# Block products for the second of eight batches, with the weights kept in DRAM one batch earlier, in an attention and gated feed-forward kernel

## The chip, the cores and the metric

The kernel runs on one core of a Trainium2 chip. The metric is device time in microseconds: the median of repeated executions of the whole program. TensorE (PE in the profile) does matrix products; VectorE (DVE), ScalarE (ACT) and GpSimd (POOL) work elementwise; SyncE (SP) issues the transfers. SBUF is the on-chip memory, PSUM holds TensorE's results in eight banks.

## What is computed

```
def sm_attn(qq, kk, vv):
    s = scale * np.matmul(qq, kk.transpose(0, 1, 3, 2))
    s = s - np.max(s, axis=-1, keepdims=True)
    a = np.exp(s)
    a = a / (np.sum(a, axis=-1, keepdims=True) + 1e-09)
    return np.matmul(a, vv)
p_packed = sm_attn(p, k, v)
attn_out = sm_attn(q, p_packed, p_packed)
x = attn_out.transpose(0, 2, 1, 3).reshape(B * S, H * D)
a = x @ w_a
b = x @ w_b
out = a * b @ w_out
```

There are 8 batches with 8 heads, 576 positions of 64 features each, 32 packed queries per head, and 512 x 1536, 512 x 1536 and 1536 x 512 weights. All data are float32.

## The kernel before

**The algebra.** The second attention's output is a2 (softmax weights, 256 rows per batch: 8 heads x 32 packed positions) times the packed values. So x @ w_a is a2 times G, where G is the packed values times w_a, and likewise for w_b. The kernel makes G (`g_tiles` or `make_g`), multiplies it with a2 (the first product, giving a and b), multiplies a by b to h, and multiplies h with w_out (the second product).

**Words.** Each float32 operand is split into a high part of type fp32r and a low part (`lo_part`, line 93: value minus high part). A product takes three passes: high x high, high x low, low x high. So for G, for a2, for h and for w_out there are tiles named `_hi`, written by ScalarE, and `_lo`, written by VectorE or GpSimd.

**Feature tiles.** The 1536 features are 12 tiles (`NFT`) of 128. For one tile and one batch the *plain* first product (`mm1`, `mm1_half`, line 406) is 24 matmuls of 288 columns. The *block* first product (`product`, line 790, and `period`, line 844) gets the same a and b from seven products of half size, three passes each: 21 matmuls of 288 columns. It needs sums and differences of the blocks of G (`make_g`, line 801; `split_g`, line 829) and of a2 (`half_sum`, line 631, steps t0 to t3 on GpSimd; `half_parts`, line 638, steps u0 to u3 on ScalarE and VectorE). The low words of the sums of a2 are `tx_lo`.

**Stages.** Batches 0 and 1 (`NB = 2`, line 56) use the plain first product, batches 2 to 7 the block one. While batch b's first product runs, the attention of batch b + 1 runs in between: `stage1` (steps S, r) and `stage2` (steps s), in an order written out by hand in strings. `START` orders the steps ahead of batch 0's first product, `PLAN_0` those beside batch 0, `PLAN` those beside batch 1, `STEPS` those beside later batches, one entry per place in a period.

**Weights.** w_a, w_b and w_out arrive as raw 64-bit pairs of words in batch 0 and are put together in three steps: A (`high_word`, ScalarE), B (`low_word`, on the engine that `WAYS` names), C (`both_words`, line 212, VectorE, the join). Step D splits a piece of w_out into its two parts. w_a and w_b stand together in the tile `w_ab` in SBUF, 6 chunks of 1 MB, while batches 0 and 1 use them. `keep_weights` (line 624) writes the chunks to DRAM (`w_kept`), three near the end of batch 0 and three in batch 1. From batch 2 on `load_kept` (line 730) reads one chunk for two feature tiles into `wr`.

**A block period.** Period n ends tile n and begins tile n + 1 in two pairs of PSUM banks, X and V:

```
product(n, 5, X), product(n + 1, 1, X), product(n + 1, 2, V)
ScalarE copies X to d; fillers; VectorE adds V to d
product(n, 3, X), product(n + 1, 6, X)
ScalarE copies X to c2; VectorE multiplies X by d: half of h; fillers
product(n, 4, V), product(n + 1, 7, V)
VectorE adds c2 to V, multiplies by d: the other half of h; fillers
```

The fillers are matmuls of a second product (`mm2_steps`, line 749), taken from a list in the numbers that `FILLS` gives (three numbers per period). They stand where the next product waits for the copy or the sum.

**Second products before.** Batch 0's second product (4 output tiles x 12 feature tiles x 3 passes = 144 matmuls, `mm2_part`) follows its first product as a block, lines 691 to 711: nine feature tiles first, the last three behind. Batch 1's (180 matmuls, 5 output tiles) begins with a block of 96 right behind its plain first product and is otherwise filler in batch 2's periods. The memory of `w_ab` and of the plain G (pool `plain`) is released at line 712, and the tiles of the block periods (pool `late`) take its place.

**The start.** `wake` (lines 588 to 592) runs matmuls of zeros in between, so that TensorE has work while the first weights arrive.

## Time and profile before

| What | Value |
|---|---|
| Median of 3 runs | 708.7 us (707.92 to 709.09) |
| Profiled execution, first to last instruction | 705.6 us |
| TensorE busy | 699.4 us, 99% |
| VectorE busy | 455.9 us, 65% |
| GpSimd busy | 417.1 us, 59% |
| ScalarE busy | 356.9 us, 51% |
| DMA moved | 102.65 MB, mean 145 GB/s |
| Chain that ended last | 91% TensorE, 4% VectorE |

The profiled execution is one run of the program; its own time in the profile is the span. Busy time is the union of an engine's instructions. Matmuls overlap (one begins before the one ahead has ended), so their durations add up to more than the time they take; the chain of waits gives groups of them with the time that the group advances. The named idle time of an engine is what it waited just before an instruction, and for whom.

### The profile page before, as it was taken

How to read it: one execution, taken by the hardware profiler on the slowest of the kernel's cores; microseconds unless marked ns; L12 is line 12 of the kernel's file. 1: busy time of each engine (PE TensorE's matmuls, PEld its weight loads, DVE VectorE, ACT ScalarE, POOL GpSimd, SP SyncE). 2: the span in 40 equal slices, each digit the busy share in tenths (PEclk: the TensorE clock that was granted, in tenths of full speed). 3: DMA queues.
4: the chain of work that ended last, by engine and by line, in shares of the span. 5: the costliest groups of instructions: out<-in, count | busy, mean ns of one | idle time of the engine just before them, and what ended most of it. 6: DMA issues, size and time to landing. Idle time of an engine off the chain costs nothing.

```text
span 705.6 us, 14386 instructions
## 1 busy us (share of the span) xinstructions
PE 699.4 (99%) x5654; PEld 582.8 (83%) x5654; DVE 455.9 (65%) x833; ACT 356.9 (51%) x719; POOL 417.1 (59%) x321
## 2 busy tenths in 40 slices
PE   9999999999999999999999999999999999999998
PEld 7888878898788888878888788888888878888886
DVE  4997765467365679566775678765785667754332
ACT  3778724554244555535554455554545446544520
POOL 1596741337254777646863589566775578856520
PEclk9999999999999999999999999999999999999999
DMA  9999986753254736356434664556145323133002
GB/s 316 380 229 297 282 233 136 252 106 93 69 141 161 170 89 172 115 139 168 119 95 124 173 161 95 131 165 173 63 123 154 106 91 119 60 124 117 1 1 75
DMA packets 179460, 102.65 MB, mean 145 GB/s; under 512 B 145728, under 2 KB 161344, under 8 KB 174016
## 3 DMA queue, kind: packets, MB, share of 16 engines
q1 hardware_dynamic: 179392, 101.73, 50.7%
q8 instruction: 44, 0.72, 0.4%
q14 instruction: 24, 0.20, 0.1%
HBM read 85.98 MB, written 15.73 MB: 144 GB/s over the span
## 4 chain that ended last, share of the span: by engine, by line
PE 91%; DVE 4%; issue 1%; DMA 1%; ACT 1%; SPq 1%; DVEq 0%
PE x L754 36%; PE m L796 28%; PE m L414 11%; PE m L440 5%; PE x L810 4%; PE s L326 2%; PE s L341 1%; PE x L396 1%; PE s L280 1%; DMA qn<-in_q_dram 1%; PE s L316 1%; DVE a_lo L93 1%; DVE part L764 0%; DVE d L878 0%; DVE w_ab L212 0%
## 5 line engine op out<-in xcount | busy, mean ns | idle before, releaser
L754 PE MATMUL x<-wo,h_hi 128*128 128x512 f32 (+1 forms) x776 | 249.4, 391 | 0.0
L93 POOL TENSOR_TENSOR h_lo<-asb,h_hi 128x576 fp32r<-128x576 f32 x95 | 139.0, 1465 | 76.0 <-ACT h_hi L841 42.8
L754 PEld LDWEIGHTS x<-wo,h_hi 128*128 128x128 f32 x776 | 140.8, 188 | 22.1 <-ACT part L762 0.8
L754 PE MATMUL x<-wo,h_lo 128*128 128x512 f32 (+1 forms) x388 | 152.2, 392 | 0.0
L93 POOL TENSOR_TENSOR G_lo<-gs,G_hi 128x640 fp32r<-128x640 f32 x72 | 113.1, 1577 | 29.6 <-ACT G_hi L831 29.4
L754 PEld LDWEIGHTS x<-wo,h_lo 128*128 128x128 f32 x388 | 72.9, 188 | 11.7
L93 POOL TENSOR_TENSOR A_lo<-gs,A_hi 128x256 fp32r<-128x256 f32 x36 | 27.2, 755 | 89.3 <-ACT A_hi L819 89.3
L878 DVE TENSOR_TENSOR d<-m,d 128x576 f32<-128x576 f32 (+1 forms) x73 | 54.1, 741 | 34.7 <-ACT d L874 33.9
L891 DVE TENSOR_TENSOR asb<-m,d 128x288 f32<-128x288 f32 x72 | 32.5, 451 | 63.2 <-ACT c L887 59.9
L887 ACT COPY c<-m 128x288 f32<-128x288 f32 x72 | 28.8, 400 | 82.5 <-PE m L796 82.5
L764 DVE TENSOR_TENSOR part<-x,part 128x512 f32<-128x512 f32 (+1 forms) x65 | 44.1, 678 | 38.8 <-PE x L754 38.8
L796 PE MATMUL m<-tx_hi,G_hi 128*128 128x288 f32 x216 | 63.8, 296 | 0.0
L796 PE MATMUL m<-tx_hi,G_lo 128*128 128x288 f32 x216 | 63.6, 295 | 0.0
L796 PE MATMUL m<-tx_lo,G_hi 128*128 128x288 f32 x216 | 63.2, 293 | 0.0
L816 ACT COPY gs<-x 128x512 f32<-128x512 f32 x35 | 20.6, 588 | 82.2 <-PE x L810 80.6
L831 ACT CAST G_hi<-gs 128x640 fp32r<-128x640 f32 x72 | 52.2, 729 | 15.7 <-POOL gs L825 15.1
L874 ACT COPY d<-m 128x576 f32<-128x576 f32 (+1 forms) x73 | 46.7, 640 | 19.2 <-PE m L796 18.8
L841 ACT CAST h_hi<-asb 128x576 fp32r<-128x576 f32 x72 | 49.0, 680 | 11.5 <-DVE asb L905 11.5
L796 PEld LDWEIGHTS m<-a_hi,G_hi 128*128 128x128 f32 x144 | 27.0, 187 | 31.9 <-issue 17.4
L825 POOL TENSOR_TENSOR gs<-gs 128x512 f32<-128x512 f32 x36 | 46.7, 1297 | 3.2 <-DVE gs L822 2.9
L796 PE MATMUL m<-a_hi,G_hi 128*128 128x288 f32 x144 | 46.6, 324 | 0.0
L904 DVE TENSOR_TENSOR m<-m,c 128x288 f32<-128x288 f32 x72 | 33.3, 463 | 17.0 <-PE m L796 15.3
(189 smaller groups left out, 1568.9 us busy)
## 6 DMA issues: line engine op xcount, KB each, us to landing
wr<-w_kept SPq DMA_DIRECT2D x36, 1024.0 KB, 5.1
nat<-in_k_dram SPq DMA_DIRECT2D x56, 144.0 KB, 4.7
nat<-in_q_dram SPq DMA_DIRECT2D x56, 144.0 KB, 5.3
vt<-in_v_dram SPq DMA_DIRECT2D x28, 256.0 KB, 3.9
out_dram<-part SPq DMA_DIRECT2D x27, 256.0 KB, 2.1
raw<-in_moe_w_a_dram SPq DMA_DIRECT2D x12, 512.0 KB, 8.7
raw<-in_moe_w_b_dram SPq DMA_DIRECT2D x12, 512.0 KB, 8.7
raw<-in_moe_w_out_dram SPq DMA_DIRECT2D x12, 512.0 KB, 6.9
```

Source lines behind the costliest of these rows:

```text
L93: return eng.tensor_tensor(out=dst, in0=src, in1=hi.bitcast(F32), op=ALU.subtract)
L414: nc.tensor.matmul(out=ps[:, half, 0:HS], lhsT=gt[:, kt, ft % 4, cols], rhs=at[:, kt, HS * half:HS * half + HS], start=(n == 0 and kt == 0 ...
L440: nc.tensor.matmul(out=o[:, cols], lhsT=ht[:, c0:c0 + P], rhs=wt[:, cols], start=(ft == 0 and n == 0), stop=(ft == NFT - 1 and n == 2))
L754: nc.tensor.matmul(out=o[:, cols], lhsT=ht[:, c0:c0 + P], rhs=wt[:, cols], start=(ft == fts[0] and n == 0), stop=end)
L764: nc.vector.tensor_tensor(out=parts[i][:, cols], in0=o[:, cols], in1=parts[i][:, cols], op=ALU.add)
L796: nc.tensor.matmul(out=bank[:, n % 2, 0:HS], lhsT=g, rhs=t, start=(first and i == 0), stop=(i == 2), skip_group_check=True)
L825: nc.gpsimd.tensor_tensor(out=gs[:, 2:4].rearrange("p a u f -> p a (u f)"), in0=gs[:, 0:2].rearrange("p a u f -> p a (u f)"), in1=s2.unsqu ...
L831: nc.scalar.copy(out=G_hi[:, n % 3], in_=gs[:, 1:6, n % 2])
L841: nc.scalar.copy(out=view(h_hi[ft]), in_=src)
L874: nc.scalar.copy(out=d[:, both], in_=X[:, both, 0:HS])
L878: nc.vector.tensor_tensor(out=d[:, both], in0=V[:, both, 0:HS], in1=d[:, both], op=ALU.add)
L904: nc.vector.tensor_tensor(out=v, in0=v, in1=c2, op=ALU.add)
```

## The change

`NB` becomes 1: batch 1 too goes through block periods, so there are seven batches of 12 block tiles. The rest follows from that:

- `w_ab` becomes six tiles. Chunks 0 and 1 lie in a pool of their own (`kp`); block periods of batch 1 use them in place (tags A and wr) and later put the parts of G's blocks (`A`) and the loaded chunks (`wr`) in their memory. Chunks 2 to 5 lie in the pool `plain`, whose memory the late tiles take.
- All six chunks are written to DRAM in batch 0, by steps K0 to K5 of `PLAN_0`.
- Batch 0's second product is nine feature tiles as a block, whose sums ScalarE copies out (`put_part`); its last three feature tiles (36 matmuls) become the first fillers.
- Batch 1's block periods get tables of their own: `STEPS_1`, and `FIRST_FILLS` for periods -2 to 11. Periods -2 and -1 begin the first tile.
- In batch 1, `GLO` and `HLO_1` put 6 of the 12 low parts of G and 5 of those of h on VectorE; the others stay on GpSimd.
- `START`, `WAYS`, `SUBS`, `MULS`, `WLO` and `PLAN_0` get other contents; the order of the first loads changes (a first weight load ahead of q's second part and of v).

```
-    NB = 2
+    NB = 1
+    kp = ep(tc.tile_pool(name="kp", bufs=1, side="right"))
...
-    w_ab = plain_p.tile([P, NC, R, 4 * P], F32, name="w_ab")
+    w_ab = [kp.tile([P, R, 4 * P], F32, name=f"w_ab{c}", tag=("A", "wr")[c]) for c in range(2)]
+    w_ab += [plain_p.tile([P, R, 4 * P], F32, name=f"w_ab{c}") for c in range(2, NC)]
...
-    SUBS, MULS, LOWS = "0101", "0100", "01"
-    HLO, WLO = "000000001000", "000011000011"
+    SUBS, MULS, LOWS = "0110", "1010", "01"
+    HLO, WLO = "000000001000", "010010000101"
...
+            elif name[0] == "K":
+                keep_weights(int(name[1]))
...
-        if n < LAST:
-            t = lp.tile([P, R, 4 * P], F32, name="wr")
+        if n < 4:
+            wr_of[n] = w_ab[n // 2]
+        elif n < LAST:
+            t = kp.tile([P, R, 4 * P], F32, name="wr", tag="wr")
...
-        lo_part(G_lo[:, n % 3], gs[:, 1:6, n % 2], G_hi[:, n % 3], nc.gpsimd)
+        lo_part(G_lo[:, n % 3], gs[:, 1:6, n % 2], G_hi[:, n % 3], nc.vector if GLO[n:n + 1] == "1" else nc.gpsimd)
...
-            lo_part(view(h_lo[ft]), src, view(h_hi[ft]), nc.gpsimd)
+            lo_part(view(h_lo[ft]), src, view(h_hi[ft]), nc.vector if HLO_1[n:n + 1] == "1" else nc.gpsimd)
...
+    F0 = 9
+    tiles = list(enumerate(tiles_of(0)))
+    pairs = [bank_pair() for _ in range(2)]
+    banks = [pairs[i % 2][:, i // 2, :] for i in range(4)]
+    for f in range(F0):
+        for i in (1, 3, 0, 2):
+            drain(mm2_steps(banks[i], tiles[i][1], [f], None, first=f == 0, last=f == F0 - 1))
+            if i in (3, 2):
+                between()
+    for i in (1, 3, 0, 2):
+        put_part(0, 0, banks[i], i, 0)
...
+    def rest_of_first():
+        for i, c0 in tiles:
+            o = bank()
+            yield from mm2_steps(o, c0, range(F0, NFT), lambda o=o, i=i, c0=c0: put_part(0, 2, o, i, c0))
+    filler[0] = rest_of_first()
...
+    GLO, HLO_1 = "101100001110", "000011010101"
+    FIRST_FILLS = ((0, 8, 6), (0, 4, 0), (4, 1, 2), (2, 0, 0), (2, 0, 2), (2, 1, 0), (0, 0, 0), (2, 0, 0), (11, 3, 8), (9, 5, 0), (6, 1, 7), (5, 5, 0), (6, 0, 14), (14, 2, 0))
...
     for n in (-2, -1):
-        period(n, (12, 12, 12), STEPS[n])
+        period(n, FIRST_FILLS[n + 2], STEPS[n])
```

**What moves, at three places.** The rows are instructions in the order in which an engine takes them; L and a number is the line in the kernel at hand, and the names left of the arrow are written, those right of it read.

The first place is TensorE at the changeover to block products, period -1: products 1 and 2 of the first tile, then what comes ahead of product 6 (`tx_hi`). Before (first tile of batch 2, two rows of the block ahead of it):

```order
L754 MATMUL x<-wo,h_hi_518 128x512 x2
L754 MATMUL x<-wo,h_lo_519 128x512
L796 MATMUL m<-a_hi,A_hi 128x288
L796 MATMUL m<-a_hi,A_lo 128x288
L796 MATMUL m<-a_lo,A_hi 128x288
L796 MATMUL m<-a_hi,A_hi 128x288
L796 MATMUL m<-a_hi,A_lo 128x288
L796 MATMUL m<-a_lo,A_hi 128x288
L754 MATMUL x<-wo,h_hi_520 128x512 x2
L754 MATMUL x<-wo,h_lo_521 128x512
L754 MATMUL x<-wo,h_hi_522 128x512 x2
L754 MATMUL x<-wo,h_lo_523 128x512
```

And now (first tile of batch 1):

```order
L686 MATMUL x<-wo,h_hi_540 128x512 x2
L729 MATMUL m<-a_hi,A 128x288 x2
L729 MATMUL m<-a_lo,A 128x288
L729 MATMUL m<-a_hi,A 128x288 x2
L729 MATMUL m<-a_lo,A 128x288
L729 MATMUL m<-tx_hi,G_hi 128x288
L729 MATMUL m<-tx_hi,G_lo 128x288
L729 MATMUL m<-tx_lo,G_hi 128x288
L686 MATMUL x<-wo,h_lo_541 128x512
```

Before, 12 fillers stood between products 2 and 6; now product 6 follows directly, and the fillers ahead of product 1 are 14 of batch 0's 36.

The second place is TensorE in period 2 of the first block batch, from the fillers behind product 2 to those at its end: products 3 (`a_hi`), 6 (`tx_hi`), 4 (`tx_hi`) and 7. Before:

```order
L754 MATMUL x<-wo,h_hi_520 128x512 x2
L754 MATMUL x<-wo,h_lo_521 128x512
L754 MATMUL x<-wo,h_hi_522 128x512 x2
L796 MATMUL m<-a_hi,G_hi 128x288
L796 MATMUL m<-a_lo,G_hi 128x288
L796 MATMUL m<-a_hi,G_lo 128x288
L796 MATMUL m<-tx_hi,G_hi 128x288
L796 MATMUL m<-tx_lo,G_hi 128x288
L796 MATMUL m<-tx_hi,G_lo 128x288
L316 MATMUL s<-ident,t_2495 128x128 x4
L317 MATMUL s<-ident,t_2495 64x128
L754 MATMUL x<-wo,h_lo_523 128x512
```

And now:

```order
L686 MATMUL x<-wo,h_hi_538 128x512 x2
L729 MATMUL m<-a_hi,G_hi 128x288
L729 MATMUL m<-a_lo,G_hi 128x288
L729 MATMUL m<-a_hi,G_lo 128x288
L729 MATMUL m<-tx_hi,G_hi 128x288
L729 MATMUL m<-tx_lo,G_hi 128x288
L729 MATMUL m<-tx_hi,G_lo 128x288
L729 MATMUL m<-tx_hi,G_hi 128x288
L729 MATMUL m<-tx_lo,G_hi 128x288
L729 MATMUL m<-tx_hi,G_lo 128x288
```

Two fillers are left behind product 2, and none stands between product 6 and product 4.

The third place is VectorE in period 0 of the first block batch, from one add of d to the next. Before:

```order
L878 TENSOR_TENSOR d<-m,d 128x576
L286 TENSOR_REDUCE nmx<-s 128x1
L287 TENSOR_SCALAR nmx<-nmx 128x1
L891 TENSOR_TENSOR asb<-m,d 128x288
L904 TENSOR_TENSOR m<-m,c_2372 128x288
L905 TENSOR_TENSOR asb<-m,d 128x288
L764 TENSOR_TENSOR part_2225<-x,part_2225 128x512
L878 TENSOR_TENSOR d<-m,d 128x576
```

And now:

```order
L813 TENSOR_TENSOR d<-m,d 128x576
L826 TENSOR_TENSOR asb<-m,d 128x288
L839 TENSOR_TENSOR m<-m,c_1589 128x288
L840 TENSOR_TENSOR asb<-m,d 128x288
L95 TENSOR_TENSOR G_lo<-gs,G_hi 128x640
L306 TENSOR_SCALAR rs<-rs,rs_1682 128x1
L307 RECIPROCAL rs<-rs 128x1
L813 TENSOR_TENSOR d<-m,d 128x576
```

The low part of G, which GpSimd made before, stands in VectorE's queue ahead of the next add of d.

## Rows read from the trace of the kernel before

**Rows 1.** The page, part 1: busy time, share of the span and instructions.
```profile
PE 699.4 (99%) x5654; PEld 582.8 (83%) x5654; DVE 455.9 (65%) x833; ACT 356.9 (51%) x719; POOL 417.1 (59%) x321
```

**Rows 2.** By stage: length; busy PE, PEld, DVE, ACT, POOL; clock; DMA share, GB/s.
```profile
28.20:80.60 52.40, 51.38 (x493) 43.61 (x492) 44.48 (x71) 40.64 (x74) 41.80 (x25) 1.00 0.97 297
80.60:118.30 37.70, 37.70 (x255) 28.60 (x253) 26.35 (x41) 16.02 (x28) 16.02 (x11) 1.00 0.76 190
118.30:167.10 48.80, 48.80 (x542) 43.69 (x541) 26.21 (x45) 24.46 (x47) 19.25 (x14) 1.00 0.60 148
...
275.00:358.00 83.00, 82.94 (x647) 69.26 (x640) 57.16 (x109) 43.71 (x91) 55.93 (x45) 1.00 0.50 134
```

**Rows 3.** Chain of waits in order of time: start us, us, what.
```profile
149.75 1.60 PE m L414 x12
...
185.99 2.78 PE x L754 x12
...
192.53 1.20 PE x L810 x16
...
215.44 1.20 PE m L796 x9
```

**Rows 4.** Groups by line, VectorE from 80.6 to 118.3: busy us, mean ns, idle before.
```profile
L212 DVE SCALAR_TENSOR_TENSOR wo_f<-raw 128x512 uint32<-128x512 uint32 x8 | 5.4, 681 | 3.2 <-POOL wo L93 2.9 <-POOL raw L206 0.2
L126 DVE STREAM_TRANSPOSE xT<-nat 128x1152 f32<-128x1152 f32 x3 | 4.0, 1348 | 0.0
L206 DVE TENSOR_SCALAR raw<-raw 128x512 uint32<-128x512 uint32 x5 | 3.2, 663 | 0.0
L93 DVE TENSOR_TENSOR wo<-wo_f,wo 128x512 fp32r<-128x512 f32 x4 | 2.9, 734 | 2.1 <-ACT wo L237 2.1
...
L366 DVE STREAM_TRANSPOSE t<-t 128x576 f32<-128x576 f32 x2 | 1.5, 774 | 1.4 <-POOL t L362 1.4
```

**Rows 5.** Groups by line over the whole span, same columns.
```profile
L93 POOL TENSOR_TENSOR h_lo<-asb,h_hi 128x576 fp32r<-128x576 f32 x95 | 139.0, 1465 | 76.0 <-ACT h_hi L841 42.8 <-ACT h_hi L433 32.3
L93 POOL TENSOR_TENSOR G_lo<-gs,G_hi 128x640 fp32r<-128x640 f32 x72 | 113.1, 1577 | 29.6 <-ACT G_hi L831 29.4
...
L878 DVE TENSOR_TENSOR d<-m,d 128x576 f32<-128x576 f32 x71 | 53.2, 749 | 30.3 <-ACT d L874 29.5
...
L874 ACT COPY d<-m 128x576 f32<-128x576 f32 x71 | 45.9, 646 | 15.9 <-PE m L796 15.5
...
L891 DVE TENSOR_TENSOR asb<-m,d 128x288 f32<-128x288 f32 x72 | 32.5, 451 | 63.2 <-ACT c L887 59.9 <-POOL G_lo L93 1.4 <-POOL h_lo L93 0.7
...
L822 DVE TENSOR_TENSOR gs<-gs,x 128x256 f32<-128x256 f32 x35 | 14.7, 421 | 1.2
```

**Rows 6.** Instructions on tiles a_lo and h_lo: duration ns min/median/max, first and last start.
```profile
L93 DVE TENSOR_TENSOR a_lo<-t,a_hi x25: 444/1036/1726, 110.1 to 607.0; 128x288 fp32r<-128x288 f32 x24, 128x576 fp32r<-128x576 f32 x1
...
L93 DVE TENSOR_TENSOR h_lo<-asb,h_hi x1: 759/759/759, 69.0 to 69.0; 128x576 fp32r<-128x576 f32 x1
```

**Rows 7.** Timeline of VectorE from 262 us: start us, us, instruction.
```profile
268.89 1.94 DVE L93 TENSOR_TENSOR tx_lo<-tf,tx_hi 128x576 fp32r<-128x576 f32 x1
...
273.65 1.73 DVE L93 TENSOR_TENSOR a_lo<-t,a_hi 128x288 fp32r<-128x288 f32 x1
...
276.16 0.45 DVE L93 TENSOR_TENSOR a_lo<-t,a_hi 128x288 fp32r<-128x288 f32 x1
```

**Rows 8.** Timeline of GpSimd in the same stretch.
```profile
273.51 1.55 POOL L93 TENSOR_TENSOR G_lo<-gs,G_hi 128x640 fp32r<-128x640 f32 x1
```

**Rows 9.** Chain of waits from 0 to 36 us.
```profile
22.24 2.49 DVE w_ab L212 x4
...
30.62 0.49 ACT ghi L402
...
31.16 3.72 PE m L414 x24
```

**Rows 10.** DMA issues: number, KB each, median us from issue to landing.
```profile
w_kept<-w_ab SPq DMA_DIRECT2D x6, 1024.0 KB, 7.1
```

More of the change, by code (lines that the diff above doesn't have):

```diff
@@ L394, in g_tiles @@
                     rows = slice(64 * e, 64 * e + 64)
-                    w = w_ab[rows, c, r, :].rearrange("p (a u f) -> p u a f", a=2, u=2)
+                    w = w_ab[c][rows, r, :].rearrange("p (a u f) -> p u a f", a=2, u=2)
                     nc.tensor.matmul(
@@ L435, in mm1 @@
         between()
-    def mm2_part(o, c0, fts, cols=slice(0, DO)):
-        for ft in fts:
-            for n, (ht, wt) in enumerate(((h_hi[ft], wo_hi[ft]), (h_hi[ft], wo_lo[ft]), (h_lo[ft], wo_hi[ft]))):
-                nc.tensor.matmul(
-                    out=o[:, cols], lhsT=ht[:, c0:c0 + P], rhs=wt[:, cols],
-                    start=(ft == 0 and n == 0), stop=(ft == NFT - 1 and n == 2))
     def store(b, ob, c0, cols=slice(0, DO)):
@@ L468, in store_first @@
             c, i, n = c + m, i + m, n - m
-    def out_tile(i):
-        if i % 3 == 1:
-            return sm.tile([P, DO], F32, name="wo_f32", bufs=1)
-        return sm.tile([P, 2, HS], F32, name="asb").rearrange("p u t -> p (u t)")[:, 0:DO]
-    def mm2_out(b, o, c0, i):
-        ob = out_tile(i)
-        nc.scalar.copy(out=ob, in_=o)
-        store(b, ob, c0)
     def drain(g):
@@ L484, in drain, with emit @@
             pass
-    def emit(b, plan, tasks={}):
+    def emit(b, plan):
         for name in plan.split():
-            if name in tasks:
-                next(tasks[name], None)
+            if name == "g":
+                g_tiles(b, (0, 1))
                 continue
@@ L665, in tiles_of, with between @@
         return [64 + P * i for i in range(4)] if b % 2 == 0 else [P * i for i in range(5)]
[L667 to L711 removed]
+    slot = [0]
+    def between():
+        emit_steps(1, PLAN_0.get(slot[0], ""))
+        slot[0] += 1
+    for ft in range(NFT):
+        if ft % 2 and ft + 1 < NFT:
+            g_tiles(0, (ft + 1, ft + 2))
+        mm1(0, ft, between)
     plain.__exit__(None, None, None)
@@ L717, in tile_packed_attn_gated_ffn @@
     G_lo = lp.tile([P, 3, 5, P], F32R, name="G_lo")
-    A_hi = lp.tile([P, E, 4, P], F32R, name="A_hi")
-    A_lo = lp.tile([P, E, 4, P], F32R, name="A_lo")
+    A_of = []
     gs = lp.tile([P, 6, 2, P], F32, name="gs")
@@ L747, in flush, with mm2_steps @@
             pend.pop(0)()
-    def mm2_steps(o, c0, fts, then, cols=slice(0, DO)):
+    def mm2_steps(o, c0, fts, then, cols=slice(0, DO), first=True, last=True):
         for ft in fts:
@@ L754, in mm2_steps @@
                 nc.tensor.matmul(
-                    out=o[:, cols], lhsT=ht[:, c0:c0 + P], rhs=wt[:, cols], start=(ft == fts[0] and n == 0), stop=end)
-                if end:
+                    out=o[:, cols], lhsT=ht[:, c0:c0 + P], rhs=wt[:, cols],
+                    start=(first and ft == fts[0] and n == 0), stop=(last and end))
+                if end and then:
                     pend.append(then)
@@ L814, in make_g @@
         flat = lambda t: t.rearrange("p x f -> p (x f)")
+        if n == 0:
+            A_of.append(kp.tile([P, 2, E, 4, P], F32R, name="A", tag="A"))
         x0, x1 = gps[0], gps[1]
         nc.scalar.copy(out=gs[:, 0:2].rearrange("p a u f -> p (a u f)"), in_=x1)
-        a_parts = [[flat(t[:, e, n % 4:n % 4 + 2]) for t in (A_hi, A_lo)] for e in range(E)]
+        a_parts = [[flat(A_of[0][:, i, e, n % 4:n % 4 + 2]) for i in range(2)] for e in range(E)]
         nc.scalar.copy(out=a_parts[0][0], in_=x0[:, 0:2 * P])
@@ L909, in period @@
         step("end")
-    paired[0] = True
-    tiles = list(enumerate(tiles_of(1)))
-    first = tiles[:3]
-    start = slot[0]
-    def block():
-        yield from mm2_third(1, 0, tiles)
-        yield from mm2_third(1, 1, tiles[:3])
-    filler[0] = block()
-    while slot[0] <= max(plan) or (slot[0] - start) % 4:
-        fill(6)
-        flush()
-        between()
+    F0 = 9
+    tiles = list(enumerate(tiles_of(0)))
+    pairs = [bank_pair() for _ in range(2)]
+    banks = [pairs[i % 2][:, i // 2, :] for i in range(4)]
@@ new lines, in tile_packed_attn_gated_ffn @@
+    for f in range(F0):
[5 more added lines that the diff above has]
+        put_part(0, 0, banks[i], i, 0)
+    while slot[0] <= max(PLAN_0):
+        between()
+    for _ in pieces:
+        emit(0, "A B C D")
+    paired[0] = True
+    def rest_of_first():
+        for i, c0 in tiles:
+            o = bank()
+            yield from mm2_steps(o, c0, range(F0, NFT), lambda o=o, i=i, c0=c0: put_part(0, 2, o, i, c0))
@@ L937, in tile_packed_attn_gated_ffn @@
             filler[0] = mm2_third(part_b, third, some)
-        period(n, FILLS[n // 2 % NFT][n % 2] if n != LAST - 3 else (4, 4, 4), STEPS[n % (2 * NFT)])
+        m = n + NFT
+        fills = FIRST_FILLS[n + 2] if n < NFT else FILLS[m // 2 % NFT][m % 2] if n != LAST - 3 else (4, 4, 4)
+        period(n, fills, STEPS_1[n] if n in STEPS_1 else STEPS[m % (2 * NFT)])
     split_h(LAST - 1)
```

82 lines of the change are left out of this document (13 added, 69 removed), and 4 rows, old and new, of the table PLAN_0.

## The prediction

> **What bounds the kernel now.** I read the page first. TensorE is busy for 99% of the span, VectorE for 65%, GpSimd for 59%, ScalarE for 51% [rows 1]. So the time is TensorE's work plus the few places where it waits. The table by stage says where those are. Batch 0's first product (28.2 to 80.6 us) loses 1.0 us; in batch 0's second product (80.6 to 118.3), in batch 1's plain first product (118.3 to 167.1) and in a later batch (275 to 358) TensorE's busy time equals the stretch to 0.1 us, and the granted clock is 1.00 everywhere, the 2.4 GHz level [rows 2]. The chain of waits then gives pitches without gaps: 12 matmuls of a plain first product in 1.60 us and 9 of a block product in 1.20 us, both 0.133 us each; 12 of a second product in 2.78 us, 0.231 each; one G step of 8 matmuls (16 records) 1.20 us [rows 3]. DMA is 97% busy until 80 us [rows 2].
>
> The profiled span is 705.6 us and the median of the runs is 708.7; the 3.1 us between them lie around the span. I sum against the span and add 3.1.
>
> **The change, part by part.**
>
> *Products of batch 1.* Removed: 12 tiles of 24 matmuls, 288. Added: 12 periods of 21, 252. Both have pitch 0.133 [rows 3], so 36 x 0.133 = **-4.8 us**. The old ones lay wholly on the path [rows 2], so nothing hid them.
>
> *G for batch 1.* Four steps of 512 columns and four of 256 become six of 512 in block form: the same columns. I take 0; one step costs 1.20 us where 512 columns are written and TensorE changes to a full-height product [rows 3], so a gain or loss up to 0.4 stays open.
>
> *Second product.* Batch 0 keeps 144 matmuls, batch 1 keeps 180. But batch 0's last three feature tiles (36 matmuls, 8.3 us) leave the middle and become filler between block products. The total is unchanged; what changes is cover, the next two terms.
>
> *The changeover (first order excerpt).* Before, 36 + 288 matmuls and a block of 96 lay between batch 1's attention and its successor's block products. Now batch 1's own attention must be split for block products right behind batch 0's nine feature tiles. TensorE gets from its last plain matmul to product 6 of tile 0 in 9 x 2.78 = 25.0, plus about 2.4 of attention matmuls (estimate from the small matmuls left over in [rows 2]: 37.7 less 144 x 0.231 and G for three tiles, 1.8), 1.0 for G, 14 fillers x 0.231 = 3.2 and products 1 and 2 (0.8): 32.4 us. VectorE's work in that stretch, by the order and the durations of [rows 4 to 7]: 8 joins of w_out x 0.681 = 5.4; 3 low words x 0.663 = 2.0; 3 low parts of w_out x 0.734 = 2.2; 4 turns of q and k x 1.348 = 5.4; batch 1's attention 9.9 (four transposes and four reductions near 0.77, a subtraction 0.76, a scaling 0.99, the rest small); two low parts of a at 1.04 (2.1), three adds for G at 0.42 (1.3), tx_lo 1.94: 30.2 us. Instructions that follow each other start some 0.07 before the one ahead ends (four joins take 2.49 us, not 4 x 0.68 = 2.72, [rows 9]), so these 41 take 27.3, and with an a_lo and G_lo behind them 28.6. VectorE starts on them 0.6 late (the last product of h is ahead), so the slack is 3.2 us. In the same stretch of before it stood idle for 11.3 us [rows 2], of which 3.2 and 2.1 ahead of steps of w_out and 1.4 ahead of attention's last transposes [rows 4]; 3 to 6 us of these remain in kind, so the stall is 0 to 3 us. I take **+0.7**, near the lower end since the new order issues attention earlier (TensorE's first s step behind 3 of the nine feature tiles, not 5); bounds 0 and 5.
>
> *Thin periods (second excerpt).* A steady block period has 12 fillers; periods 0 to 5 of batch 1 have 7, 2, 4, 3, 0, 2 matmuls. Without filler, product 3 waits until ScalarE has copied d out of X: from product 1's last start I allow 0.2 us for its end, the copy takes 0.646 [rows 5], product 2 covers 0.40: some 0.46 stays open, two fillers. The tables give two almost everywhere, and attention matmuls in period 4. What is left is VectorE's queue. Between the adds of d in periods 3 and 4 it has the add of d (0.75), two turns x 1.35, two products of h and the sum of V (0.45 each, like L891), reciprocals (0.4) and three adds for G (1.3) [rows 4, 5]: 6.5 us, against 5.2 of TensorE. Product 2 of tile 5 needs V free, which comes some 5.3 us after period 3's first block, where TensorE is at 4.3: 1.0 us. Tile 0's uncovered copy costs 0.3, and smaller ones 0.5: **+1.8**. Below, 0.5, if VectorE runs ahead; above 5, if each of six periods lost 0.8 (0.46 and a late sum).
>
> *Low parts moved to VectorE (third excerpt).* Of batch 1's 24 low parts of G and h, 11 go from GpSimd (1.58 and 1.47 us, [rows 5]) to VectorE, where one such h_lo took 0.759 [rows 6]. But that one ran beside nothing to be shared. The same operation on 288 columns takes 0.444 to 1.726 us [rows 6], and the timeline shows why: the 1.73 us one begins at 273.65 inside GpSimd's G_lo (273.51 for 1.55) and ends 0.32 after it; one at 276.16, when that G_lo is over, takes 0.45 [rows 7, 8]. Five of the 11 fall in thin periods; others stand beside 10 to 22 fillers. GpSimd is busy for half to two thirds of such a period, so two or three of the five wait some 0.6; half reaches TensorE: **+0.4**, bounds 0 and 3. The Trainium skill, "SBUF — State Buffer", section "SBUF: two separate sides", calls the port pair of VectorE and GpSimd an exclusive lock: a VectorE operation with two SBUF inputs and a GpSimd operation exclude each other for a whole instruction. By that rule, which the trace bears out in [rows 7, 8], all five would wait and this term would be the rival's, not 0.4; it speaks against the move.
>
> *Weights written to DRAM earlier.* Six writes of 1 MB, 7.1 us each to landing [rows 10], move from 100 to 130 us to batch 0's last tiles. Their memory is next written when the partial sums are copied out, 25 us behind the last but one; SP's loads for batch 2 queue behind them and are needed only 20 us later. 0; without that cover up to 2.
>
> *Batch 0's steps and the start.* Same number of joins before the first G, same number of dummy matmuls (61). Before, the first product began at 31.16 behind VectorE's chain and ScalarE's ghi, while dummies filled TensorE until then [rows 9]. One join now fills a gap of 1.0 us ahead of the first transpose, but a 0.5 MB weight load stands ahead of v. I take 0, bounds -0.7 and +0.7. From batch 2 on, the tables are the old ones: 0.
>
> Sum: -4.8 + 0.7 + 1.8 + 0.4 = **-1.9**: span 703.7, time **706.8 us**. Its own range is 705.4 to 708.3. A measurement of this kernel can tell about 0.2%, 1.4 us, so faster means below 707.3.
>
> **The rivals.**
> - *All hidden.* VectorE keeps ahead, periods lose 0.5 or less: -4.8 to -4, about 704.2. For: GpSimd and ScalarE are far from full, and steady periods lose nothing [rows 2]. Against: those have 12 fillers. Chance 0.25.
> - *Slower: the changeover waits for VectorE.* One mechanism: tx_lo and G_lo of tile 0 come behind w_out's last pieces on VectorE. It decides once VectorE's waits in the 32.4 us exceed 3.2 + 2.6 us, when the stall of 2.6 uses up the 0.7 and the 1.9 of the sum. With all 11.3 us of before [rows 2] the stall would be 8.1 and the time 708.7 - 4.8 + 8.1 + 2.2 = 714.2; with 8.5, 5.3 and 711.4. Chance 0.20.
> - *The shared port rules the thin periods.* All five moved parts wait, about 1 us each on average, and product 2 waits for V each time: the terms 1.8 and 0.4 become 4.4: 708.7 - 4.8 + 0.7 + 4.4 = 709.0. For: [rows 7, 8]. Against: moving work off GpSimd also leaves it fewer operations to collide with. Chance 0.15. The lock in the Trainium skill's "SBUF — State Buffer" (same section) is this mechanism.
> - My forecast has 0.40.
>
> That the change doesn't do what it says is excluded: the order shows the 36 matmuls gone.
>
> **How the numbers follow.** The range takes the all-hidden case with 0.7 from the start (703.4) and reaches into the late changeover up to 711.5; some 0.1 lies on each side. Faster: 0.25, of the forecast 0.29 (it falls under 707.3 in three of four): 0.54. Same: 0.11 of the forecast, 0.07 of the port, 0.02 of the changeover: 0.20. Slower: 0.08 and 0.18: 0.26.
>
> **What would show it.** In the changed profile: 288 plain first-product matmuls, not 576, and 1764 block ones. The start of batch 2's first block period should come about 1.9 us earlier than its 192.53 us now [rows 3]; all later stages should keep their lengths of 83 us per batch [rows 2]. TensorE's waits should stand in two places: behind batch 0's ninth feature tile, released by VectorE's tx_lo, wo or G_lo, and about block period 3 to 4, released by VectorE's product of h. VectorE's moved low parts should range from 0.76 to 2 us, long where GpSimd runs. I am wrong if batch 2 begins later than 192.53, if later stages change their length, or if the start alone moves by over a microsecond.

## The result and the profile after

The changed kernel takes **715.5 us** (median of five runs, 712.4 to 717.1) against 708.7: 1.0095 times, with a 95% interval of 1.0075 to 1.0115. It is slower, by 6.8 us, and 4.0 us beyond the upper end of the range. The profiled execution is the fastest of the five, 710.6 us from first to last instruction, 5.0 more than before. What follows explains these 5.0 us; the other 1.8 are not in this profile, and the last section says what goes with them. Of all executions behind this document two, both of the edit e19 below, took 1450 and 1458 us, for a cause that no run shows, and the figures of e19 leave them out.

Part 1 of the page after, to be held against [rows 1]:

```profile
PE 698.2 (98%) x5586; PEld 576.2 (81%) x5586; DVE 484.1 (68%) x895; ACT 369.1 (52%) x752; POOL 438.3 (62%) x338
```

TensorE does 68 matmul records less and is busy for 1.2 us less, in a longer span: it waits more. The groups by line count 288 plain first-product matmuls and 1764 block ones, as foretold. The table by stage, columns as in [rows 2]: batch 0's first product with what lies just ahead, batch 0's nine feature tiles, batch 1's block periods, a later batch.

```profile
28.20:85.60 57.40, 53.25 (x495) 43.95 (x493) 48.07 (x74) 39.72 (x72) 44.93 (x26) 1.00 0.98 275
85.60:114.60 29.00, 28.75 (x189) 21.73 (x188) 22.84 (x38) 14.59 (x27) 15.35 (x13) 1.00 1.02 316
114.60:198.60 84.00, 81.61 (x681) 65.15 (x688) 66.31 (x125) 48.96 (x105) 44.53 (x37) 1.00 0.55 142
281.00:364.00 83.00, 82.93 (x642) 69.28 (x640) 57.27 (x110) 43.94 (x92) 55.83 (x44) 1.00 0.50 134
```

Batch 0's first product lost 1.0 us before [rows 2] and loses 4.2 now. The later batch is as it was. The DMA engines are full to 114 us, where [rows 2] had 0.76 from 80.6 on.

The chain of waits, in order of time:

```profile
54.34 5.57 DMA raw<-in_moe_w_b_dram
...
59.93 0.52 DVE raw L208
60.45 2.86 DVE w_ab L214 x2
...
84.53 5.31 DMA vt<-in_v_dram
...
138.40 5.22 DMA wr<-w_kept
...
198.81 0.86 PE x L743 x16
```

The last row is the G step that stood at 192.53 in [rows 3]: 6.3 us later, not 1.9 earlier. The other rows are transfers on the path, where before DMA was 1% of the chain and is now 5%: a weight piece, batch 1's v, and the weights' reload.

To share the 5.0 us out I took each matmul shape's usual pitch (start to next start) in the trace of before as its work. The rest of the time holds the waits, and also the small matmuls and the changes of shape, so that it isn't zero where TensorE never stood; only its difference counts:

| stretch | before | after | difference |
|---|---|---|---|
| start to the first product | 31.2 | 32.6 | +1.4 |
| first product of batch 0 | 48.8 | 53.0 | +4.1, all in the rest |
| from there to the G step above | 112.4 | 113.0 | +0.7: work 99.7 to 94.7, rest 12.6 to 18.3 |
| behind it | 513.3 | 512.0 | -1.2 |

Of the 5.7 us in the third row, 1.7 stand at the changeover, 1.7 in the G step of period 4, 0.6 at batch 1's v, and some 0.9 in the other G steps; what is left is in small pieces. The fourth row shrinks by 0.6 us in small even steps and by 0.3 to 0.4 at either end; no run tells why.

### The profile page after: what moved, and what is told of

It reads as the page before. It is cut to its first block, busy times and chain, and to the rows that moved or that the text cites. A ratio compares the mean times of both kernels' runs of the same rounds, so it can differ in the third digit from the quotient of the medians.

```text
span 710.6 us, 14404 instructions
## 1 busy us (share of the span) xinstructions
PE 698.2 (98%) x5586; PEld 576.2 (81%) x5586; DVE 484.1 (68%) x895; ACT 369.1 (52%) x752; POOL 438.3 (62%) x338
## 4 chain that ended last, share of the span: by engine, by line
PE 84%; DVE 6%; DMA 5%; issue 2%; ACT 2%; SPq 1%; POOL 0%; DVEq 0%; ACTq 0%; POOLq 0%
PE x L686 36%; PE m L729 32%; PE x L743 5%; PE m L686 3%; PE m L416 3%; DMA vt<-in_v_dram 2%; PE s L328 2%; DMA raw<-in_moe_w_a_dram 1%; PE s L343 1%; DVE w_ab L214 1%; DVE a_lo L95 1%; PE s L282 1%; DMA raw<-in_moe_w_b_dram 1%; PE s L318 1%; DMA wr<-w_kept 1%
## 5 line engine op out<-in xcount | busy, mean ns | idle before, releaser
L686 PE MATMUL x<-wo,h_hi 128*128 128x512 f32 (+1 forms) x800 | 258.1, 391 | 0.0
L95 POOL TENSOR_TENSOR G_lo<-gs,G_hi 128x640 fp32r<-128x640 f32 x78 | 122.7, 1579 | 31.4 <-ACT G_hi L766 31.1
L95 POOL TENSOR_TENSOR A<-gs,A 128x256 fp32r<-128x256 f32 x42 | 31.5, 751 | 99.0 <-ACT A L754 94.8
L813 DVE TENSOR_TENSOR d<-m,d 128x576 f32<-128x576 f32 (+1 forms) x85 | 63.1, 742 | 37.6 <-ACT d L809 36.9
L729 PE MATMUL m<-a_hi,A 128*128 128x288 f32 x336 | 80.3, 297 | 0.1
L729 PE MATMUL m<-tx_hi,G_hi 128*128 128x288 f32 x252 | 74.7, 297 | 1.4 <-ACT d L809 1.3
L729 PE MATMUL m<-tx_hi,G_lo 128*128 128x288 f32 x252 | 74.2, 295 | 0.0
L729 PE MATMUL m<-tx_lo,G_hi 128*128 128x288 f32 x252 | 73.8, 294 | 0.0
L766 ACT CAST G_hi<-gs 128x640 fp32r<-128x640 f32 x84 | 60.9, 730 | 17.1 <-POOL gs L760 16.5
L729 PEld LDWEIGHTS m<-a_hi,A 128*128 128x128 f32 x336 | 58.7, 188 | 0.8 <-DVE asb L840 0.6
## 6 DMA issues: line engine op xcount, KB each, us to landing
raw<-in_moe_w_a_dram SPq DMA_DIRECT2D x12, 512.0 KB, 8.1
raw<-in_moe_w_b_dram SPq DMA_DIRECT2D x12, 512.0 KB, 8.3
raw<-in_moe_w_out_dram SPq DMA_DIRECT2D x12, 512.0 KB, 6.1
```

The source lines that it names most:

```text
L95: return eng.tensor_tensor(out=dst, in0=src, in1=hi.bitcast(F32), op=ALU.subtract)
L686: nc.tensor.matmul(out=o[:, cols], lhsT=ht[:, c0:c0 + P], rhs=wt[:, cols], start=(first and ft == fts[0] and n == 0), stop=(last and end))
L729: nc.tensor.matmul(out=bank[:, n % 2, 0:HS], lhsT=g, rhs=t, start=(first and i == 0), stop=(i == 2), skip_group_check=True)
L766: nc.scalar.copy(out=G_hi[:, n % 3], in_=gs[:, 1:6, n % 2])
L813: nc.vector.tensor_tensor(out=d[:, both], in0=V[:, both, 0:HS], in1=d[:, both], op=ALU.add)
```

## The experiments

Seventeen edits and the changed kernel again, each in four to twelve executions. The kernel before, run beside them, had medians of 708.2 to 708.5. "Ends" is the start of the last matmul of batch 0's first product in the profile (80.0 before, 85.6 after). The half writes of e7 and e18 leave later batches without their right weights: they measure time alone.

| run | edit | median (range), us | ends |
|---|---|---|---|
| c_again | none | 717.2 (714.0 to 718.2) | 85.2 |
| e1 | v later | 717.5 (715.1 to 719.5) | 84.1 |
| e2 | old start | 720.9 (720.2 to 722.5) | 84.1 |
| e3 | e1 and e2 | 719.9 (716.4 to 721.7) | 88.0 |
| e4 | kernel before, v first | 711.6 (710.2 to 712.1) | 83.7 |
| e11 | v and query later | 714.6 (713.1 to 715.5) | 81.4 |
| e5 | key behind u0, u1 | 716.7 (714.4 to 719.5) | 83.3 |
| e7 | half writes | 715.0 (713.8 to 715.6) | 85.6 |
| e18 | e11, half writes | 709.3 (708.1 to 712.0) | 81.8 |
| e15 | e11, key later | 715.6 (713.1 to 717.7) | 81.5 |
| e16 | e15, sums on VectorE | 715.7 (714.8 to 716.7) | 81.8 |
| e17 | e16, reload first | 713.2 (711.5 to 714.0) | 81.6 |
| e8 | reload first | 714.3 (712.4 to 714.8) | 83.4 |
| e6 | tile closed, period 3 | 716.4 (712.0 to 717.8) | 83.8 |
| e12 | tile closed earlier | 716.0 (712.8 to 718.2) | 82.3 |
| e14 | e11, e8, e12, u3 later | 715.3 (713.9 to 718.6) | 83.3 |
| e19 | e11, e8, key behind the last weights | 710.8 (709.5 to 712.5) | 82.4 |
| e20 | e19, writes behind the key | 712.3 (710.6 to 713.3) | 84.0 |

### The changed kernel again

> The changed kernel itself, unaltered, timed beside the edits below so that they are compared with it on the same chip: 714 to 717 us against a kernel before of 708 to 709. If the loss comes from arrivals in the early part, its runs spread over 3 us or more while those of the kernel before spread over 1 to 2, and this profile has its largest early waits at other places or of other lengths than the 2.9 us at 60.3 of the first profile; if the loss is VectorE's work, the waits are the same to 0.3 us.

Both kernels spread as expected (4.2 us here, 1.8 for the 11 runs of before). The early waits moved: the G step at 60 us took 3.9 us in the first profile and 1.4 in this one (1.1 in the kernel before), the first product began at 33.3, a v load cost 0.4 at 89. Yet the product ended at 85.2. In these two profiles, where TensorE waits differs more than how much.

### The order of the loads

VectorE in the changed kernel, with its idle time before each instruction in brackets:

```profile
56.64 1.38 DVE L128 STREAM_TRANSPOSE xT<-nat 128x1152 f32<-128x1152 f32 x1 [1.56 <-DMA nat<-in_k_dram]
...
59.93 0.52 DVE L208 TENSOR_SCALAR raw<-raw 128x512 uint32<-128x512 uint32 x1 [0.83 <-DMA raw<-in_moe_w_b_dram]
60.37 2.94 DVE L214 SCALAR_TENSOR_TENSOR w_ab<-raw 128x512 uint32<-128x512 uint32 x2
```

and SyncE's queue ahead of it (start, us until the next could be issued):

```profile
41.43 1.44 SPq L172 DMA_DIRECT2D vt<-in_v_dram  x2
42.91 2.55 SPq L176 DMA_DIRECT2D vt<-in_v_dram  x2
45.56 0.38 SPq L224 DMA_DIRECT2D raw<-in_moe_w_a_dram  x1
45.99 7.46 SPq L120 DMA_DIRECT2D nat<-in_k_dram  x4
53.55 0.69 SPq L224 DMA_DIRECT2D raw<-in_moe_w_a_dram  x1
54.34 0.93 SPq L224 DMA_DIRECT2D raw<-in_moe_w_b_dram  x2
```

The joins that TensorE waited for at 60.3 us stand behind two arrivals. The weights' last piece landed at 61.7 us, where before it landed at 57.5: v's loads went ahead of it (the key's slow ones did so before, too). e1, e2 (before's `FIRST`, `START`, `WAYS`, `SUBS`, `MULS`), e3 and e4:

```diff
-B C A A B C A Lv0 C Lk1 | ... | A B C T0 |
+B C A A B C A C Lk1 | ... | A B C T0 Lv0 |
```

> The changed kernel, with the four loads of batch 1's v (1 MB) issued in slot 7 of batch 0's steps and not in slot 0, ahead of nothing that batch 0 needs. Theory A (arrivals): the 16 DMA engines are full until 80 us, a 512 KB weight piece lands every 1.35 us, so the v loads push the second half of batch 1's key and the last three weight pieces 2.6 us back; VectorE waits 1.56 us for that key and 0.83 us for a piece, the joins of the fifth weight chunk come late, and TensorE stands 2.9 us in the G step at 60.3 us. Then that wait falls below 0.7 us and the time by 2 to 3 us, from a median of 715.5 to about 713. Theory B (VectorE's longer work and the low parts that GpSimd gave up are the loss, the loads are hidden): within 0.7 us of 715.5, the wait at 60.3 stays.

> The changed kernel with the order of first loads, the start's steps and the tables of the start's engines as before. Theory C (start): v's first half lands at 13.0 us and not 9.8, because a weight piece was put ahead of it, and one of the products by the softmax's sums went to GpSimd (1.17 us beside some 0.7 on VectorE), so the first product begins at 32.6 us and not 31.2: the time falls by 1 to 1.8 us, to about 714. Theory A: the wait in the G step at 60.3 us stays at 2 to 3 us, since the v loads of batch 1 still go ahead. Theory B: within 0.7 us of 715.5, start hidden.

> Both edits together: batch 1's v loads in slot 7, and the start's loads and steps as before. Theories A and C add up: 3.5 to 5 us less than the changed kernel, a median of about 711, the first product at 31.2 us and no wait over 0.7 us in the G step near 60 us. What is then left above 704 to 705 (4.8 us of products saved from 708.7) is the changeover and the thin periods. Theory B: 715 and a loss that begins only behind 114 us.

> The kernel before, with batch 1's first v loads put into slot 0 of batch 0's steps, ahead of the second half of batch 1's key (they stood in slot 5). Theory A: the weights' last pieces land 2.6 us later, as in the changed kernel, and TensorE waits 1.5 to 3 us for a join near 60 us: 710.2 to 711.7 against 708.7. Rival: the kernel before has the slack to take it, 708.7 within 0.7, and the wait of the changed kernel comes from its own order of the conversions.

e4 went as theory A says: in the kernel before, v's loads ahead of the key alone cost 3.3 us, this wait at 55 us for the key's transposition among them:

```profile
PE s L280 <- DVE xT L126: 1.6, 1, 1.6
```

In the changed kernel the same edit undone gained nothing (e1). The wait at 60.3 went, though it had gone from c_again's profile without an edit, so that e1 doesn't show why. In its place stood this:

```profile
PE s L328 <- DMA vt<-in_v_dram: 2.3, 2, 2.0
```

(TensorE's waits in e1, 28 to 118 us: in total, times, longest.) The second v half, which shares its buffer with one still in use, was issued at 82.7 behind four output weights and landed at 91; TensorE was there at 87.6. e2 and e3 began the first product at 32.2 and 30.9 us and were the slowest of all: before's start does not fit this kernel's order of batch 0. So theory A was incomplete, and theory C's gain did not reach the end.

e11 also moves the query:

```diff
-| A Lq1 | ... | C B A B S1 K2 |
+| A | ... | C B A B Lq1 S1 K2 |
```

> The changed kernel with v's first half (slot 0 to 7) and the second half of the query (slot 6 to 17) of batch 1 loaded about where the kernel before loads them, behind more of the weights. Theory A, second form: with only the v loads moved the wait went from the G step at 60 us to the second v half at 87.6 us, because the last four pieces of the output weights, which stand behind the query's slow loads (9 us of issue, 71 to 80), and then that v half land at 84 to 91. With the query behind them they land 4 to 5 us earlier, the wait at 87.6 goes too, and batch 0's first product ends by 82 us (85.5 in the changed kernel, 80.0 before): 3 to 4 us less than the changed kernel, 712 to 713.5. Rival (the bound is the conversions or the start, not the order of the loads): the end of that product stays at 84 to 85.5 and the time within 1 us.

The first product ends at 81.4, 4.2 us earlier, and the wait for v is gone. Where the loss shows differs from profile to profile: the product ends at 82.3 to 85.6 in the seven with the changed loads (after, c_again, e5 to e8, e12) and at 81.4 to 83.3 in the seven with e11's (e11, e14 to e19). At the last matmul of the nine feature tiles, behind the waits for v, they are apart: it starts at 113.5 to 118.2 us in the first seven (114.3 in both profiles of the changed kernel) and at 110.1 to 112.4 in the others (110.6 in e11). So the order of these loads costs some 3.7 us up to there. The time fell by only 2.6 us against c_again. TensorE's waits from 110 to 118 us in e11, and VectorE there:

```profile
PE x L686 <- ACT wo L239: 2.7, 1, 2.7
```

```profile
109.46 1.38 DVE L128 STREAM_TRANSPOSE xT<-nat 128x1152 f32<-128x1152 f32 x1 [3.51 <-DMA nat<-in_k_dram]
112.86 1.38 DVE L128 STREAM_TRANSPOSE xT<-nat 128x1152 f32<-128x1152 f32 x1 [2.02 <-DMA nat<-in_k_dram]
114.16 0.79 DVE L95 TENSOR_TENSOR a_lo<-t,a_hi 128x288 fp32r<-128x288 f32 x2
114.86 0.68 DVE L214 SCALAR_TENSOR_TENSOR wo_f<-raw 128x512 uint32<-128x512 uint32 x1
```

VectorE waits 5.5 us for batch 2's key, with the last output weights' join (L214) behind it, and TensorE needs those weights.

### The weight writes and what waits behind them

That key is loaded behind the six writes K0 to K5. In SyncE's queue of the changed kernel:

```profile
92.57 4.47 SPq L590 DMA_DIRECT2D w_kept<-w_ab  x4
97.14 13.36 SPq L120 DMA_DIRECT2D nat<-in_k_dram  x8
```

These four writes land at 98.8 to 106.2 us, 2.5 us apart, the key's loads from 106.8 to 112.8.

e5 (`k2` behind `u0 u1`) and e7 (512 KB per write, each reload reading it twice):

> One order changed at the end of batch 0: the transposition of batch 2's first key half stands behind the splits u0 and u1, not ahead of them. Theory K (the early weight writes): six writes of 1 MB push that key's load back, it lands at 112.8 us, VectorE waits 2.1 us for it, and the splits behind it come late, which is what TensorE waits for at 119.6 us (1.46) and 122.4 (0.28). Then the splits fill that wait, the two waits of TensorE fall below 0.5 us together and the time by 1 to 1.8 us. Theory V (VectorE has too much work at the changeover, the key's arrival costs nothing): the same work in another order, within 0.5 us of the changed kernel.

> The six writes of weights to DRAM in batch 0 are cut to 512 KB each, and each later load reads that half twice (the later batches' weights are then not the reference's). Theory K: 3 MB less in the full queue, batch 2's key lands some 7 us earlier, VectorE's wait of 2.1 us for it goes and with it TensorE's waits at 119.6 and 122.4: 1 to 1.8 us less than the changed kernel; the waits before 86 us, where the first write starts, stay. Rival (my prediction's term: these writes cost nothing): within 0.5 us.

e5 changed nothing beyond the spread, and the wait at the changeover stayed at 1.6 us: theory K was wrong there. e7 brought the key from 112.8 to 106.5 us and took VectorE's wait for it away, and the changeover's wait still stayed:

```profile
PE m L731 <- ACT d L811: 1.3, 1, 1.3
```

It is ScalarE's copy of d, which stands behind its split of G, and that behind GpSimd's part of G (1.2 us waited for). ScalarE in e7:

```profile
120.00 0.73 ACT L768 CAST G_hi<-gs 128x640 fp32r<-128x640 f32 x1 [1.20 <-POOL gs L762]
120.63 0.43 ACT L609 CAST a_hi<-t 128x288 fp32r<-128x288 f32 x1
120.96 0.43 ACT L609 CAST tx_hi<-tf 128x288 fp32r<-128x288 f32 x1
121.30 0.39 ACT L811 COPY d<-m 128x288 f32<-128x288 f32 x1
```

By time e7 is 2.2 us below c_again and 0.5 below the first five executions; the ranges overlap, so no gain is shown.

e18 has the loads of e11 and the half writes; e15 has e11's loads and this:

```diff
-D C s1 D s0 Lk2 s1 t0 k3 t1 Lq3 t2 | | k2 t3 | | u0 | Lq2 Lv2 D
+D C s1 D s0 Lk2 s1 t0 t1 t2 | | t3 | | u0 | D k3 Lq3 k2 Lq2 Lv2
```

> The loads as in e11, and the transpositions of batch 2's key (both halves, with the query loads that reuse their memory) behind the last of batch 0's conversions and the splits u0. Theory K (queue behind the key): VectorE's 3.5 and 2.0 us of waiting for the key no longer stand ahead of the last output weights, TensorE's 2.9 and 0.5 us at 113 to 117 us go, 2.5 to 3.5 us less than e11: about 711.5, and the changeover's 1.5 us for d's copy may come back, then 712.5. Rival: the last weights' own arrival or ScalarE sets that wait, and it stays: 714.5.

> e11 with the six early writes halved to 512 KB (later batches' weights are then not the reference's). If the writes are what makes the key late, it lands some 6 us earlier (106.5 us for 112.8, as the half writes gave without e11's edit), VectorE's 5.5 us of waiting shrink below 1 us, and TensorE's wait at 113 us goes below 0.5 us with no change of order: 711.5 to 712.5. Rival: as above, 714.5.

e18 is the clearest step of all: 709.3 against 714.6 for e11, and the ranges don't overlap (708.1 to 712.0, 713.1 to 715.5). VectorE in e18:

```profile
105.37 2.60 DVE L128 STREAM_TRANSPOSE xT<-nat 128x1152 f32<-128x1152 f32 x2
107.89 1.85 DVE L95 TENSOR_TENSOR a_lo<-t,a_hi 128x288 fp32r<-128x288 f32 x2
109.66 0.68 DVE L214 SCALAR_TENSOR_TENSOR wo_f<-raw 128x512 uint32<-128x512 uint32 x1
```

The transpositions no longer wait, and the join comes at 109.7, not 114.9. TensorE's waits of 2.9 and 1.0 us at 113 and 91.7 are gone. Three megabytes of writes (7.4 us at the 2.45 us in which one megabyte landed) cost 5.3 us here.

That price is more than these two waits. In e18's profile the reload's wait at 143 (0.9 us in e11) is gone too, and the changeover's 1.5 us, which e11 had lost, came back. Most of the remainder goes with TensorE's clock: in e11 it stood at 0.50, the 1.2 GHz level, from 117.9 to 121.3, right behind the wait at 113, in e18 at 1.00. One stretch, first in e11, then in e18 (the clock is the third number from the end):

```profile
118.00:121.00 3.00, 3.00 (x10) 2.30 (x8) 3.00 (x5) 1.83 (x5) 1.31 (x2) 0.50 0.98 239
118.00:121.00 3.00, 2.90 (x39) 1.25 (x38) 2.17 (x5) 0.78 (x2) 1.55 (x1) 1.00 0.37 87
```

Half of that stretch, 1.7 us, is an estimate of what it took. By mean clock: 0.995 to 0.998 in e11's six executions, 1.000 in eight of e18's twelve; at 0.998 e11 took 713.1 and 713.2 us, e18 710.9, 710.9 and 712.0. So about 2 of the 5.3 us remain at equal clock.

e15 gained nothing because the last join still stood behind the key (it is emitted after all slots). e19 puts it ahead (`D C D k3 ...`), with e8's edit; e20 also moves the writes among the loads:

> The loads as in e11, the v loads behind the reload as in e8, and at the end of batch 0's steps the last output weights' joining and splitting (and u0) ahead of the transpositions of batch 2's key. If the cost of the writes is what waits in VectorE's queue behind the late key, TensorE's 2.3 to 2.9 us at 113 us go, the changeover's 1.5 us for d's copy comes back: 711 to 712.5, against 714.5 for e11. If it is the transfers themselves, a wait of 1.5 us or more stays between 88 and 117 us and the time above 712.5.

> e19 with the same six writes in another order among the loads: the first behind batch 1's second query half, two of the last behind batch 2's key halves, and the second chunk's at the end. The key lands 4 to 6 us earlier and the query 2 us earlier, so the 0.8 to 1.2 us at 91.7 us go too: 709.5 to 711, close to the 709.3 of halved writes. If the writes cost by their volume, wherever they stand, it stays at 711 to 713.

TensorE's waits in e19, 28 to 200 us:

```profile
PE m L729 <- ACT d L809: 1.8, 1, 1.8
PE m L416 <- ACT ghi L404: 1.7, 1, 1.7
PE s L343 <- DVE ppT L263: 1.0, 1, 1.0
PE x L743 <- ACT gs L751: 0.8, 1, 0.8
```

At 710.8 us e19 is 3.8 below e11, 0.2 below the range given for "what queues behind the key", and the wait at 113 us is gone; the changeover's came back with 1.8 us. Part of the 3.8 is e8's edit: against e17, which has it too, e19 is 2.4 below. In e20 the key came earlier and the wait at 91.7 went, but the second chunk's write now landed at 126.5 us and the reload into its memory behind it: a new wait of 3.0 us at 131.8. So the writes did not lose their price in either of the two places that were tried.

### The start

> e15 with the start's differences and products by the sums on the engines that had them before (the product of 1.17 us back from GpSimd to VectorE). Theory C, cut to this part: GpSimd stands 0 to 2.2 us for a weight piece with that product queued behind, so the first product begins at 32.3 to 34.6 us from run to run; it begins at 31.2 to 31.8, its spread below 1 us, 1 to 2 us less than e15. Rival: v's late landing (13.0 us for 9.8) sets the start, which then stays at 32.3 or later.

Refuted: the first product began at 32.6 us, as with GpSimd's product (32.2 to 34.6 in the fourteen profiles with the changed start, 32.4 in e17, which has e16's sums; 30.9 to 32.2 in four with the old start). The order of the first loads alone was not tried, so which part of the start costs the 1.4 us stays open.

### The thin periods

e8 issues batch 2's v behind the reload (`Lv1` from period 0 to period 2); e6 and e12 move fillers:

```diff
-(2, 0, 2), (2, 1, 0), (0, 0, 0), (2, 0, 0)
+(2, 0, 2), (2, 1, 2), (0, 0, 0), (0, 0, 0)    e6
+(2, 0, 2), (5, 0, 0), (0, 0, 0), (0, 0, 0)    e12
```

> The changed kernel, with the loads of batch 2's second v half issued behind the weights' reload of period 2, not ahead of it. Theory R (reload): the one buffer that the weights come back into is free at 135.4 us, but its 1 MB load stands behind two v loads and four stores in SyncE's queue, is issued at 138.4 and lands at 143.6, where the G step of period 4 would start at 142.4 to 143.2; the landing is then 1.5 to 2 us earlier and the 0.4 to 1.2 us that TensorE waits ahead of that G step go; the 1.33 us in the middle of the same step stay. By the time: 0.4 to 1.2 us less than the changed kernel's 715.5 to 717.2, which its spread of 3 to 4 us may cover. Rival: the wait is not the landing, and stays.

> The last two of the 36 fillers go from period 5 to period 3, so that no second-product tile is open while the G step of period 4 runs. Theory F: an open tile holds one of the two banks that the G step needs, so its second eight matmuls wait 1.33 us for ScalarE's copy of the first; the wait at 144.2 us goes, the time falls by 0.8 to 1.4 us (a little is given back in period 5, which has no filler left). Rival: the wait comes from the weights' late landing at 143.6 us and stays; within 0.4 us.

> The last five fillers all stand at the head of period 3, and periods 4 and 5 have none; in the built kernel the two halves of period 4's G step now have two banks, where they shared one, also when the tile was closed only at the end of period 3. Theory F again, with the bank held until VectorE's sum and not only until the last matmul: the 1.33 us in the middle of that G step go, and 0.5 us or less comes back where periods 4 and 5 have no filler: 0.8 to 1.4 us less. Rival: it was hidden behind another wait of the same length, and the time stays within 0.4 us.

TensorE's waits from 142 to 147 us, c_again and then e8:

```profile
PE x L743 <- DMA wr<-w_kept: 1.0, 1, 1.0
PE x L743 <- ACT gs L751: 0.8, 1, 0.8
```

```profile
PE x L743 <- ACT gs L751: 0.8, 1, 0.8
```

Theory R holds. By time e8 is 2.9 us below c_again and e17 2.6 below e16, more than the wait itself. The clock goes with the excess: its mean is 0.995 to 1.000 in e8 and 0.998 to 1.000 in e17, but 0.990 to 0.995 in four of c_again's five and 0.995 to 0.998 in e16; no run separates the two. The second row is the bank: an open tile of the second product holds one of two banks, both halves of period 4's G step stand in the other, and the second waits for ScalarE's copy of the first. (The rows count idle time alone; from matmul to matmul it is 1.33 us, and so are the figures in the text.) e6 left that unchanged, which fits a bank held until VectorE's sum and not only until the last matmul; in e12, where the tile closes earlier, the wait is gone. The time is not: 1.4 us at the next G step's reload and 0.8 for VectorE's product of h took its place, the wait that I had foretold for this stage. In e12:

```profile
PE x L743 <- DMA wr<-w_kept: 1.6, 2, 1.0
PE m L729 <- DVE asb L840: 0.7, 1, 0.7
```

> All of it: the loads as in the run before this one, the v loads behind the reload, the tile closed early, and u3 behind d's copy in period -1, since at the changeover TensorE waits for ScalarE's copy of d, which stands behind three splits and those behind GpSimd's part of G (1.46 to 1.6 us in every run so far, also where VectorE's work there was put in another order). Expected: the waits in period 4's G step gone (2 to 2.5 us), the changeover's 1.5 us down to 0.7 to 1, and the early part 3 to 4 us shorter: 707.5 to 710 us. If the early part is bound by something else than the order of these loads: 712.5 to 714. Theory V (VectorE's longer work): above 714.

e14 missed at 715.3: it still had 3.2 us behind the late key, 2.9 us ahead of the first product (1.5 in the kernel before), and e12's new waits. The key hid the changeover's wait, so moving u3 remains untested.

> e16 with the v loads of batch 2 behind the weights' reload in period 2, as in e8. All early causes are then taken away and only the thin periods' waits are left, G step of period 4 with its one bank (1.33 us) and d's copy (1.5 us) the largest: 708.5 to 710.5 us. If it stays above 711.5, the early part has one more bound that I have not named.

713.2, above its 711.5: the bound not named was the last join behind the key, which e19 then took away.

## Why the prediction was wrong

**Products, -4.8: right.** TensorE's work to the G step fell by 5.0.

**Batch 0's steps and the start, 0 (+-0.7): the step that failed.** 1.4 us at the start and 4.1 in the first product, together more than the 5.0 by which the profile grew. I counted joins and dummy matmuls, not the loads that move past weights in SyncE's queue, though [rows 2] showed the DMA engines 97% busy there. e4 shows the mechanism in the kernel before (+3.3), e11 undoes it (3.7 us at the last of the nine feature tiles). My own criterion, a start moving by over a microsecond, was met; what moved the start stays open.

**Weights written earlier, 0 ("without that cover up to 2"): failed too, behind the first.** I looked for who needs the loads behind the writes and found batch 2's use of its key 20 us later. But the key's transposition stands in VectorE's queue, ahead of work for batch 0 and batch 1; its wait is theirs. As changed it cost VectorE 2.1 us (2.7 in c_again) without a cost in time that e7 could show, since TensorE was late anyway. With the loads in order, half of the writes' volume is worth 5.3 us (e18 against e11), the lower clock behind the stall included.

**The changeover, +0.7: place right, engine wrong.** TensorE waits 1.46 us behind the ninth feature tile and 0.28 later, within the bounds; but for ScalarE's d, not VectorE. Waits of 1.0 to 2.0 us stand there in every run with block periods in batch 1 but e11, e14 and e15, where TensorE had just been held up for 2.3 us or more.

**Thin periods, +1.8: size right by luck, cause wrong.** In period 4 stand 1.33 us for a bank and 0.4 to 1.2 (the changed kernel's two profiles) for the reload, one of four that the change adds; I had named neither. VectorE's product of h showed only in e12 and e14, when these were gone.

**G, 0 (0.4 left open): too low.** From first matmul to what follows, the G steps of this stretch took 6.5 us before and 8.8 now, of which 1.33 is the bank: some 0.9 more.

**Moved low parts, +0.4: no wait of TensorE stands behind them.** Nine of the 11 took 0.76 to 0.86 us, one 1.07, one 1.80. Two of them in VectorE's timeline:

```profile
154.95 0.76 DVE L95 TENSOR_TENSOR h_lo<-asb,h_hi 128x576 fp32r<-128x576 f32 x1
...
158.45 1.80 DVE L95 TENSOR_TENSOR h_lo<-asb,h_hi 128x576 fp32r<-128x576 f32 x1
```

The first began when a GpSimd split had 0.03 us to go, the second inside GpSimd's work on gs, which had begun at 158.34 and took 1.29. The rule of the Trainium skill ("SBUF — State Buffer", section "SBUF: two separate sides"), that the two engines keep each other off their shared port, agrees: only three of the 11 began inside a GpSimd instruction with 0.1 us or more to go, and they took 0.86, 1.07 and 1.80. The rival that the port would rule the thin periods does not hold, since the others met none or only its edge.

**Rivals.** "Slower: the changeover waits for VectorE" has the sign and nearly the size, but not the mechanism. The right one, transfers displacing each other in a full queue, was not among them.

## What to carry to other kernels

- Where the DMA engines are full, as they were here to 114 us, count no transfer as free: write down what lands later when one is moved, and for each late landing the in-order queue whose head waits for it. The victim here was what stood behind that wait, not the transfer's own user.
- A wait that goes is a gain only if nothing else was due then. e1, e5, e12 and e14 each removed or aimed at a wait of 1 to 3 us and gained little, since another arrival was as late. Read the whole chain again after each edit.
